# Sliding-window attention with sink tokens into a maxout FFN on one core: more zero products at the start, one cast on ScalarE, and a new order of the first five chunks

## The chip, the cores and the metric

The kernel runs on one core of a Trainium2 chip. The metric is the device time of one execution in microseconds. Before the change three runs took 179.35, 179.66 and 179.69 us, a median of 179.66. Five engines work side by side, each through its own list of instructions in order, and wait for one another by semaphores: PE (TensorE, matrix products; its weight loads are the row PEld), DVE (VectorE), ACT (ScalarE), POOL (GpSimd) and SP (SyncE, which here only issues DMAs).

## The reference

Attention over 4 batches, 8 heads, 768 positions and a head dimension of 64: a query sees the 128 positions up to its own, and the first 4 positions (the sinks). The result, 3072 tokens by 512, goes through an FFN whose hidden layer is the maximum of three products.

```python
scores = scale * np.matmul(q, k.transpose(0, 1, 3, 2))
is_sink = pos[None, :] < int(n_sink)                  # n_sink = 4
rel = pos[:, None] - pos[None, :]
in_window = (rel >= 0) & (rel < int(window))          # window = 128
scores = np.where(is_sink | in_window, scores, -1000000000.0)
a = softmax(scores)
x = np.matmul(a, v)                                   # tokens x 512, heads side by side
h = np.maximum(np.maximum(x @ w1, x @ w2), x @ w3)    # 512 -> 768
out = h @ w_out                                       # 768 -> 512
```

Inputs and output are float32 in device memory; the kernel computes in bf16 with float32 sums.

## The kernel before, in words

**Chunks.** The work is cut into 12 chunks of 256 positions of one batch (3 chunks a batch), each with all 8 heads, taken as 4 pairs of heads. For a chunk the kernel does the following.

- `load` (line 76) brings q, k and v as float32, 512 KB each, by SP's DMA queue. `part` and `parts` cut a load into halves of the heads (head pairs 0 and 1, and 2 and 3). A `gate` is a small POOL write into the target (a memset, or a copy from a weight tile) for which the DMA must wait; so POOL's place in its order decides when the load may be issued. The raw tiles have two buffers a kind.
- `cast_qk` (95) casts one half of q or k to bf16 on the engine that it is given, `cast_v` (104) a quarter of v.
- `turn` (109) and `turn2` (129) transpose one half of q or k on PE, four products with the identity, and copy the result from PSUM to qT or kT on the engine given. From chunk 4 on `turn_dma` (150) does it by DMA.
- `premask` (251) puts an additive mask into the score banks by two products with the identity ahead of the scores; `score` (259) computes the transposed scores of a pair; `expo` (282) takes the exponential on ACT, in two halves; `mask` (289) multiplies by 0 and 1 on DVE where no premask was put. `sink_k`, `sink_score`, `sink_v` (224, 294, 310) treat the four sink positions for chunks 1 and 2 of a batch.
- `av_open` and `av` (324, 338) multiply with v and a column of ones; DVE takes the reciprocal of the sums and scales (355, 358). `xpose` (362) transposes the result for the FFN.
- `ffn_h(ci, fp, wi)` (381) is one group of 8 products: chunk ci, columns 256 fp to 256 fp + 255 of hidden layer matrix wi. For wi = 0 the result is copied to h_sb (397), for 1 and 2 DVE takes the maximum (401). `ffn_y` (407) is the output product, six products of 512 columns, and a copy; `store` writes out.

**The weights** are cast on the way by POOL's own DMA queue, in nine parts of 256 columns (`load_w`, 234) and the output matrix in two (`load_wo`, 242).

**PSUM.** There are 8 banks, handed out first in, first out in the order of the program text (`bank` and `give`, 57 and 63). So the order of the text also decides whose release a bank's next user waits for.

**The order** of the first three chunks and a part of chunks 3 and 4 is written out by hand (454 to 660), call by call; each call adds to the lists of its engines. The chunks behind follow a loop (661). The text's order counts on each engine separately: two calls that share no engine and no bank can change places without a difference.

**Zeros.** `warm(n)` (172) has PE multiply n times a tile of zeros, 512 columns each, into a bank that nobody reads. The kernel does five such products at the start, and four more behind the first turn and premask.

Of the kernel before, what the change touches and what calls it, by code (L numbers as in the profile page):

```python
# [16 lines left out]
def kernel(  # L17
# [13 lines left out]
    nc = tc.nc  # L31
# [17 lines left out]
    with tc.manual_schedule():  # L49
# [13 lines left out]
        def give(*banks):  # L63
            for x in banks:
                free.append(home.pop(id(x))[1])
# [10 lines left out]
        def load(ci, what="kqv", gate=None, part=None, parts=1):  # L76
            if ci >= NCH:
                return
            b, c = divmod(ci, CPB)
            t0 = c * 256  # L80
            for w in what:
                src = {"k": k, "q": q, "v": v}[w]
                if (ci, w) not in raws:
                    raws[ci, w] = raw.tile([128, H, 2, D], F32, tag=w + "_raw", name=w + "_raw")
                dst = raws[ci, w]
                if gate is not None:
                    gate(dst[0:1, 0, 0, 0:1])
                n = H // parts
                for g in range(parts) if part is None else (part,):
                    nc.sync.dma_start(  # L90
                        out=dst[:, n * g:n * g + n],
                        in_=src[b, n * g:n * g + n, t0:t0 + 256]
                            .rearrange("h (p i) d -> p h (i d)", i=2))

        def cast_qk(ci, w, g, eng):

            if (ci, w) not in bfs:
                bfs[ci, w] = raw.tile([128, NP, 2, 2, D], BF16, tag=w + "_bf", name=w + "_bf")
            x, y = bfs[ci, w], raws[ci, w]
            f = eng.copy if eng is nc.scalar else eng.tensor_copy  # L100
            f(x[:, 2 * g:2 * g + 2].rearrange("q p i a d -> q p a i d"),  # L101
              y[:, 4 * g:4 * g + 4].rearrange("q (p a) i d -> q p a i d", a=2))
# [6 lines left out]
        def turn(ci, w, g, eng=None):  # L109

            pt = bank([128, 4, 128], BF16, "pt")
            x = bfs[ci, w]
            for i in range(4):
                y = x[:, 2 * g + i // 2, i % 2]
                nc.tensor.transpose(pt[:, i], y.rearrange("s a d -> s (a d)"), ident)  # L115
            eng = eng or (nc.scalar if w == "q" else nc.vector)
            f = eng.copy if eng is nc.scalar else eng.tensor_copy
            if w == "q":
                f(
                    qT[ci % RING][:, 2 * g:2 * g + 2].rearrange("q p i n r -> q (p i) (n r)"), pt)  # L120
            else:
                f(
                    kT[ci % RING][:, :, 2 * g:2 * g + 2].rearrange("q n p i r -> q n (p i) r"),
                    pt.rearrange("q x (n r) -> q n x r", r=64))
            give(pt)
# [46 lines left out]
        def warm(n):  # L172

            if n:
                pw = bank([128, 512], F32, "warm")
                for _ in range(n):
                    nc.tensor.matmul(pw, lhsT=wz[:, 0:128], rhs=wz, start=True, stop=True)  # L177
                give(pw)
# [103 lines left out]
        def expo(ci, p):  # L282
            lo = 0 if ci % CPB else 1
            e, st = es[ci, p]
            for a in range(2):
                nc.scalar.activation(e[:, a, lo:], st[a][:, lo:], AF.Exp, scale=scale)  # L286
                give(st[a])
# [164 lines left out]


        load(0, 'q', part=1, parts=2)
        warm(5)
        load(0, 'k')
        load(0, 'q', part=0, parts=2)
        load(0, 'v', part=0, parts=2, gate=pool_gate)
        load(0, 'v', part=1, parts=2)
        masks()  # L460
        sink_init()
        factors(msk, addm)
        cast_qk(0, 'q', 1, nc.scalar)
        turn(0, 'q', 1, nc.scalar)
        premask(0, (2,))
        warm(4)
        cast_qk(0, 'k', 1, nc.vector)
        cast_qk(0, 'k', 0, nc.gpsimd)
        cast_qk(0, 'q', 0, nc.gpsimd)
        turn(0, 'k', 1, nc.vector)  # L470
        load(1, 'k')
        premask(0, (3,))
        turn(0, 'k', 0, nc.scalar)
        score(0, (2,))
        score(0, (3,))
        turn(0, 'q', 0, nc.vector)
# [8 lines left out]
        load(1, 'v')  # L485
        score(0, (0,))
        expo(0, 3)
        premask(0, (1,))
        score(0, (1,))
        expo(0, 0)  # L490
        cast_qk(1, 'k', 0, nc.gpsimd)
        load_w(0, 256, 512)
        expo(0, 1)
        av_open(0)
        av(0, 2)
        av(0, 3)
# [3 lines left out]
        cast_qk(1, 'q', 0, nc.gpsimd)  # L500
        cast_qk(1, 'q', 1, nc.scalar)
        turn(1, 'k', 1, nc.scalar)
        av(0, 1)
        premask(1, (0,))
        premask(1, (1,))
        turn2(1, 'q', 0, nc.vector)
        turn(1, 'q', 1, nc.scalar)
        sink_k(0)
        cast_v(1, 0, 0, nc.vector)
        cast_v(1, 1, 0, nc.vector)  # L510
        load_w(0, 0, 256)
        load_w(1, 512, 768)
        score(1, (0,))
        score(1, (1,))
        expo(1, 0)
        expo(1, 1)
        xpose(0, 0, nc.vector)
        xpose(0, 1, nc.vector)
        cast_v(1, 1, 1, nc.gpsimd)
        load_w(1, 256, 512)  # L520
        cast_v(1, 0, 1, nc.gpsimd)
        load_w(1, 0, 256)
        sink_v(0)
        sink_score(1)
        score(1, (3,))
        load(2, 'k', part=0, parts=2, gate=after(0, 300))
        load(2, 'k', part=1, parts=2)
        ffn_h(0, 2, 0, 1, nc.vector)
        expo(1, 3)
        score(1, (2,))  # L530
        expo(1, 2)
        load(2, 'q', part=1, parts=2)
        load(2, 'q', part=0, parts=2, gate=pool_gate)
        load_w(2, 0, 256)
        load_w(2, 256, 512)
        load_w(2, 512, 768)
        mask(1, 3)
        ffn_h(0, 1, 0)
        mask(1, 2)
        av_open(1)  # L540
        cast_qk(2, 'k', 1, nc.gpsimd)
        av(1, 0)
        av(1, 1)
        ffn_h(0, 0, 0)
        load(2, 'v', gate=after(0, 300))
        av(1, 3)
        av(1, 2)
        ffn_h(0, 2, 1)
        ffn_h(0, 1, 1)
        xpose(1, 0, nc.vector)  # L550
        xpose(1, 1, nc.scalar)
        ffn_h(0, 0, 1)
        ffn_h(1, 2, 0)
        cast_qk(2, 'k', 0, nc.scalar)
        ffn_h(1, 1, 0)
        ffn_h(1, 0, 0)
        load_wo()
        load(3, 'q', gate=after(2, 300))
        load(3, 'k')
        factors(msk0, addm0)  # L560
        turn(2, 'k', 0, nc.vector)
        ffn_h(1, 1, 1)
        turn(2, 'k', 1, nc.scalar)
        cast_v(2, 1, 0, nc.gpsimd)
        cast_qk(2, 'q', 1, nc.scalar)
        ffn_h(1, 0, 1)
        cast_qk(2, 'q', 0, nc.vector)
        ffn_h(1, 2, 1)
        turn(2, 'q', 1, nc.scalar)
# [3 lines left out]
        score(2, (0,))  # L573
        expo(2, 0)
        score(2, (3,))
        mask(2, 0)
        score(2, (1,))
        sink_score(2)
        ffn_h(0, 1, 2)
        cast_v(2, 1, 1, nc.gpsimd)  # L580
        load(3, 'v', gate=after(1))
        cast_v(2, 0, 0, nc.gpsimd)
        cast_v(2, 0, 1, nc.gpsimd)
        expo(2, 3)
        expo(2, 1)
        ffn_h(1, 0, 2)
        ffn_h(0, 2, 2)
        ffn_h(1, 2, 2)
        score(2, (2,))
        load(4, 'q', gate=after(0, 300))  # L590
        cast_qk(3, 'q', 0, nc.gpsimd)
        mask(2, 1)
        av_open(2)
        expo(2, 2)
        ffn_y(0, 0)
        load(4, 'k', gate=after(0))
        load(4, 'v')
        cast_qk(3, 'k', 0, nc.gpsimd)
        cast_qk(3, 'k', 1, nc.scalar)
        mask(2, 3)  # L600
        mask(2, 2)
        cast_qk(3, 'q', 1, nc.vector)
        av(2, 0)
        ffn_y(0, 1)
        turn(3, 'q', 0, nc.scalar)
        av(2, 2)
        load(5, 'q')
        av(2, 3)
        turn(3, 'q', 1, nc.scalar)
        load(5, 'k', gate=after(0, 300))  # L610
        av(2, 1)
        ffn_y(1, 0)
        turn(3, 'k', 1, nc.scalar)
# [2 lines left out]
        xpose(2, 1, nc.vector)  # L616
        ffn_y(1, 1)
        cast_qk(4, 'q', 1, nc.vector)
        cast_v(3, 1, 1, nc.gpsimd)
        cast_v(3, 0, 0, nc.gpsimd)  # L620
        cast_v(3, 0, 1, nc.gpsimd)
        score(3, (1,))
        cast_qk(4, 'q', 0, nc.vector)
        expo(3, 1)
        score(3, (0,))
        cast_qk(4, 'k', 1, nc.gpsimd)
        mask(3, 1)
        cast_v(4, 1, 0, nc.gpsimd)
        ffn_h(2, 0, 0)
        cast_qk(4, 'k', 0, nc.vector)  # L630
        score(3, (3,))
        cast_v(3, 1, 0, nc.vector)
        turn_dma(4, 'k')
        turn_dma(4, 'q')
        store(0)
        store(1)
        score(3, (2,))
        expo(3, 0)
        expo(3, 3)
        ffn_h(2, 0, 2)  # L640
        mask(3, 0)
        mask(3, 3)
# [4 lines left out]
        mask(3, 2)  # L647
        av(3, 0)
        av(3, 1)
        ffn_h(2, 2, 0)  # L650
        load(5, 'v', gate=pool_gate)
        ffn_h(2, 1, 1)
        av(3, 3)
        ffn_h(2, 2, 1)
        av(3, 2)
        ffn_h(2, 2, 2)
        cast_v(4, 0, 0, nc.gpsimd)
        cast_v(4, 0, 1, nc.gpsimd)
        cast_v(4, 1, 1, nc.gpsimd)
        ffn_h(2, 1, 2)  # L660
        for i in range(3, NCH):
            n, m = i + 1, i - 1
# [153 lines left out]
```

## Time and profile before

| what | us |
|---|---|
| median of three runs | 179.66 (179.35 to 179.69) |
| the profiled execution | 178.26 |
| its span, first to last instruction | 176.5 |
| PE busy | 168.6 (96%) |
| DVE, ACT, POOL busy | 120.5, 86.4, 66.2 |
| HBM read and written | 25.17 MB and 6.29 MB |

The span is shorter than the execution by what lies ahead of the first and behind the last instruction. Busy times of one engine are those of its work, not of its waits; PE's products overlap, and their ends are modelled. A row of the timeline has the start and the length in us, the engine, the line of the code, the operation with the tile written and the tiles read, the shape, and how many instructions in a row it stands for; in brackets comes the time that the engine was idle before it, and what ended that. The row of a DMA issue is the issuing; a row of the DMA view adds the time from the issue to the landing.

### The profile page before, as it was taken

To read this page: it belongs to the slowest core of one execution; us is meant where nothing else is said; L and a number is where in the kernel's file an instruction comes from. 1 tells how busy PE (TensorE), PEld (TensorE's weight loads), DVE (VectorE), ACT (ScalarE), POOL (GpSimd) and SP (SyncE) were. 2 spreads that over 40 slices of the span, in tenths; PEclk is the share of its full clock that TensorE was granted. 3 is DMA by queue.
4 is the path that set the end of the run, shared out by engine and by line. 5 is a ranking of instruction groups with operands and counts; after the bars stand their busy time and mean duration, and the time that the engine had idled before them with its cause. 6 is when DMAs were issued, how large, how long until landed. Compare 5 with 4: busy or idle time off the path is not lost.

```text
span 176.5 us, 4618 instructions
## 1 busy us (share of the span) xinstructions
PE 168.6 (96%) x1855; PEld 126.5 (72%) x1867; DVE 120.5 (68%) x263; ACT 86.4 (49%) x173; POOL 66.2 (38%) x127
## 2 busy tenths in 40 slices
PE   5978999999999999999999999999999999999992
PEld 1546789867686687597696696796795795796871
DVE  3178764796697895775775874875785775976361
ACT  4197726766953914914724814814616616420210
POOL 7589407455293584074172145244253000000000
PEclk9999999999999999999999999999999999999998
DMA  5999999999999999997998999999999215203203
GB/s 156 297 281 198 204 214 234 217 299 287 290 188 301 304 205 198 262 236 202 258 198 219 251 182 248 260 159 243 276 163 245 32 28 156 119 4 59 119 2 119
DMA packets 70693, 34.90 MB, mean 198 GB/s; under 512 B 26640, under 2 KB 69136, under 8 KB 70672
## 3 DMA queue, kind: packets, MB, share of 16 engines
q1 hardware_dynamic: 64976, 31.33, 79.4%
q0 software_dynamic: 5552, 3.15, 12.6%
q8 instruction: 14, 0.23, 0.6%
q10 hardware_dynamic: 144, 0.13, 0.2%
q14 instruction: 7, 0.06, 0.1%
HBM read 25.17 MB, written 6.29 MB: 178 GB/s over the span
## 4 chain that ended last, share of the span: by engine, by line
PE 85%; DVE 8%; ACT 2%; issue 2%; DMA 2%
PE h_ps L390 49%; PE y_ps L411 17%; PE o L350 6%; PE st L274 6%; DVE h_sb L401 2%; PE pt L115 2%; DVE x_sb L358 2%; DMA q_raw<-in_q_dram 2%; ACT e_sb L286 1%; DVE vb L105 1%; PE o L332 1%; PE warm L177 1%; DVE e_sb L292 1%; PE xt L371 1%; PE y_ps L421 1%
## 5 line engine op out<-in xcount | busy, mean ns | idle before, releaser
L390 PE MATMUL h_ps<-xT,w 128*128 128x256 bf16 x864 | 101.7, 273 | 0.1
L390 PEld LDWEIGHTS <-w 128*128 128x128 bf16 x864 | 81.8, 98 | 10.7 <-issue 0.8
L401 DVE TENSOR_TENSOR h_sb<-h_sb,h_ps 128x512 bf16<-128x512 bf16 (+1 forms) x74 | 49.2, 670 | 17.8 <-PE h_ps L390 16.0
L286 ACT ACTIVATE e_sb<-st 128x512 bf16<-128x512 f32 (+1 forms) x96 | 46.4, 583 | 6.7 <-PE st L274 6.7
L397 ACT CAST h_sb<-h_ps 128x512 bf16<-128x512 f32 x35 | 20.6, 588 | 47.2 <-PE h_ps L390 47.0
L105 POOL CAST vb<-v_raw 64x512 bf16<-64x512 f32 x42 | 27.2, 647 | 19.3 <-DMA v_raw<-in_v_dram 17.9
L411 PE MATMUL y_ps<-wo,h_sb 128*128 128x512 bf16 x126 | 31.9, 380 | 0.6
L292 DVE TENSOR_TENSOR e_sb<-e_sb,msk 128x1024 bf16<-128x1024 bf16 (+1 forms) x42 | 27.0, 679 | 2.8 <-ACT e_sb L286 2.6
L101 POOL CAST k_bf<-k_raw 128x512 bf16<-128x512 f32 x19 | 11.8, 637 | 41.1 <-DMA k_raw<-in_k_dram 32.3
L411 PEld LDWEIGHTS <-h_sb 128*128 128x128 bf16 x138 | 12.4, 98 | 14.4 <-issue 1.6
L358 DVE TENSOR_TENSOR x_sb<-o,rc 128x256 bf16<-128x256 f32 x48 | 20.4, 424 | 1.7
L413 DVE COPY y_sb<-y_ps 128x512 f32<-128x512 f32 x13 | 9.0, 691 | 14.2 <-PE y_ps L411 14.1
L350 PE MATMUL o<-vb,e_sb 128*128 128x65 bf16 x352 | 16.8, 193 | 0.9 <-DVE vb L105 0.9
L350 PEld LDWEIGHTS <-e_sb 128*128 128x128 bf16 x352 | 14.7, 97 | 2.9 <-ACT e_sb L286 1.1
L274 PE MATMUL st<-qT,kT 64*128 64x128 bf16 (+1 forms) x256 | 14.6, 238 | 0.6 <-DVE qT L141 0.4
L274 PEld LDWEIGHTS <-kT 64*128 64x128 bf16 x256 | 8.5, 94 | 7.5 <-issue 5.1
L101 POOL CAST q_bf<-q_raw 128x512 bf16<-128x512 f32 x17 | 10.3, 627 | 5.0 <-DMA q_raw<-in_q_dram 4.9
L355 DVE RECIPROCAL rc<-o 128x4 f32<-128x4 f32 x48 | 8.4, 175 | 4.0 <-PE o L350 3.9
L306 ACT ACTIVATE e_sink<-sk 128x256 bf16<-128x256 f32 x8 | 3.1, 389 | 14.4 <-PE sk L300 14.4
L413 ACT COPY y_sb<-y_ps 128x512 f32<-128x512 f32 x10 | 5.8, 585 | 3.2 <-PE y_ps L411 2.9
L237 POOL DMA_DIRECT2D w<-in_moe_w_dram x9 | 7.0, 786 | 0.0
L177 PE MATMUL warm<-wz 128*128 128x512 bf16 x9 | 4.2, 631 | 1.2 <-DVE wz L166 1.2
(67 smaller groups left out, 71.5 us busy)
## 6 DMA issues: line engine op xcount, KB each, us to landing
k_raw<-in_k_dram SPq DMA_DIRECT2D x11, 512.0 KB, 4.9
v_raw<-in_v_dram SPq DMA_DIRECT2D x11, 512.0 KB, 7.1
out_dram<-y_sb SPq DMA_DIRECT2D x11, 512.0 KB, 3.2
q_raw<-in_q_dram SPq DMA_DIRECT2D x10, 512.0 KB, 6.4
w<-in_moe_w_dram POOLq DMA_DIRECT2D x9, 256.0 KB, 6.4
q_raw<-in_q_dram SPq DMA_DIRECT2D x4, 256.0 KB, 7.4
wo<-in_moe_w_out_dram POOLq DMA_DIRECT2D x2, 384.0 KB, 7.9
v_raw<-in_v_dram SPq DMA_DIRECT2D x2, 256.0 KB, 5.1
```

The lines of the kernel that those rows point to most:

```text
L101: f(x[:, 2 * g:2 * g + 2].rearrange("q p i a d -> q p a i d"), y[:, 4 * g:4 * g + 4].rearrange("q (p a) i d -> q p a i d", a=2))
L105: eng.tensor_copy(vb[ci % RING][64 * i:64 * i + 64, n, :, 0:D], raws[ci, "v"][64 * n:64 * n + 64, :, i])
L274: nc.tensor.matmul(st[a][:, s:s + q1 - q0].rearrange("q n (i r) -> q n i r", i=2), lhsT=x[hp, n, p].rearrange("q i r -> q (i r)"), rhs=qc[ ...
L286: nc.scalar.activation(e[:, a, lo:], st[a][:, lo:], AF.Exp, scale=scale)
L292: (eng or nc.vector).tensor_mul(e[:, :, lo:], e[:, :, lo:], msk0 if lo else msk)
L350: nc.tensor.matmul(o[:, t, a], lhsT=e[:, a, s], rhs=vb[cv % RING][:, n, 2 * p + a], start=first, stop=True, skip_group_check=True)
L358: nc.vector.tensor_mul(xs[ci][:, :, p], o[:, :, :, 0:D], rc.unsqueeze(3).to_broadcast([128, 2, 2, D]))
L390: nc.tensor.matmul(hp[:, f].rearrange("q (i t r) -> q i t r", i=2, t=2), lhsT=w_sb[wi][:, ds, c0:c0 + 128], rhs=xTs[ci][:, :, ds].rearrang ...
L397: (nc.scalar.copy if eng is nc.scalar else eng.tensor_copy)(dst, hp)
L401: nc.vector.tensor_max(dst[:, x], dst[:, x], hp[:, x])
L411: nc.tensor.matmul(yp, lhsT=hs[ci][:, fb, t * 128:(t + 1) * 128], rhs=wo[:, fb], start=(fb == 0), stop=(fb == FB - 1))
L413: (nc.scalar.copy if eng is None else eng.tensor_copy)(ys[ci][:, t], yp)
```

## The change

It makes the first group of zeros eight products instead of five, and puts the second group ahead of the mask products of pair 2 instead of behind them. The first half of chunk 0's k is cast on ScalarE instead of GpSimd, and turned ahead of the mask products of pair 3. The rest are changes of place: casts, turns, sink steps, weight loads, exponentials, AV products, groups of h and y of chunks 0 to 4. Everything else, the loop behind included, is the same. On PE the three zeros are the only instructions more; SP's list is the same.

```diff
         load(0, 'q', part=1, parts=2)
-        warm(5)
+        warm(8)
...
         load(0, 'v', part=0, parts=2, gate=pool_gate)
+        cast_qk(0, 'q', 1, nc.scalar)
         load(0, 'v', part=1, parts=2)
...
-        cast_qk(0, 'q', 1, nc.scalar)
         turn(0, 'q', 1, nc.scalar)
+        warm(4)
         premask(0, (2,))
-        warm(4)
+        cast_qk(0, 'k', 0, nc.scalar)
         cast_qk(0, 'k', 1, nc.vector)
-        cast_qk(0, 'k', 0, nc.gpsimd)
-        cast_qk(0, 'q', 0, nc.gpsimd)
         turn(0, 'k', 1, nc.vector)
         load(1, 'k')
+        turn(0, 'k', 0, nc.scalar)
+        cast_qk(0, 'q', 0, nc.gpsimd)
         premask(0, (3,))
-        turn(0, 'k', 0, nc.scalar)
...
+        load_w(0, 0, 256)
         av(0, 1)
         premask(1, (0,))
+        turn2(1, 'q', 0, nc.vector)
+        sink_k(0)
         premask(1, (1,))
-        turn2(1, 'q', 0, nc.vector)
         turn(1, 'q', 1, nc.scalar)
-        sink_k(0)
         cast_v(1, 0, 0, nc.vector)
         cast_v(1, 1, 0, nc.vector)
-        load_w(0, 0, 256)
         load_w(1, 512, 768)
+        xpose(0, 0, nc.vector)
         score(1, (0,))
         score(1, (1,))
         expo(1, 0)
         expo(1, 1)
-        xpose(0, 0, nc.vector)
+        load_w(1, 256, 512)
+        cast_v(1, 1, 1, nc.gpsimd)
         xpose(0, 1, nc.vector)
-        cast_v(1, 1, 1, nc.gpsimd)
-        load_w(1, 256, 512)
         cast_v(1, 0, 1, nc.gpsimd)
         load_w(1, 0, 256)
-        sink_v(0)
+        score(1, (3,))
         sink_score(1)
-        score(1, (3,))
         load(2, 'k', part=0, parts=2, gate=after(0, 300))
         load(2, 'k', part=1, parts=2)
+        sink_v(0)
+        expo(1, 3)
         ffn_h(0, 2, 0, 1, nc.vector)
-        expo(1, 3)
...
         av_open(1)
-        cast_qk(2, 'k', 1, nc.gpsimd)
+        ffn_h(0, 0, 0)
         av(1, 0)
-        av(1, 1)
-        ffn_h(0, 0, 0)
         load(2, 'v', gate=after(0, 300))
         av(1, 3)
+        av(1, 1)
         av(1, 2)
...
         ffn_h(0, 0, 1)
+        cast_qk(2, 'k', 1, nc.gpsimd)
         ffn_h(1, 2, 0)
         cast_qk(2, 'k', 0, nc.scalar)
+        ffn_h(1, 0, 0)
         ffn_h(1, 1, 0)
-        ffn_h(1, 0, 0)
...
         turn(2, 'k', 0, nc.vector)
+        ffn_h(1, 0, 1)
+        cast_v(2, 1, 0, nc.gpsimd)
+        turn(2, 'k', 1, nc.scalar)
         ffn_h(1, 1, 1)
-        turn(2, 'k', 1, nc.scalar)
-        cast_v(2, 1, 0, nc.gpsimd)
         cast_qk(2, 'q', 1, nc.scalar)
-        ffn_h(1, 0, 1)
...
+        ffn_y(0, 0)
+        ffn_y(0, 1)
         av(2, 0)
-        ffn_y(0, 1)
         turn(3, 'q', 0, nc.scalar)
+        cast_qk(3, 'k', 1, nc.scalar)
...
         score(3, (0,))
+        cast_qk(4, 'k', 0, nc.vector)
         cast_qk(4, 'k', 1, nc.gpsimd)
         mask(3, 1)
+        ffn_h(2, 0, 0)
         cast_v(4, 1, 0, nc.gpsimd)
-        ffn_h(2, 0, 0)
-        cast_qk(4, 'k', 0, nc.vector)
```

More of the change, by code (lines that the diff above doesn't have):

```diff
@@ L487 @@
         expo(0, 3)
+        cast_qk(1, 'k', 0, nc.gpsimd)
         premask(0, (1,))
@@ L490 @@
         expo(0, 0)
-        cast_qk(1, 'k', 0, nc.gpsimd)
+        expo(0, 1)
         load_w(0, 256, 512)
-        expo(0, 1)
         av_open(0)
@@ L534 @@
         load_w(2, 0, 256)
+        expo(1, 2)
         load_w(2, 256, 512)
@@ L575 @@
         score(2, (3,))
-        mask(2, 0)
         score(2, (1,))
+        cast_v(2, 1, 1, nc.gpsimd)
         sink_score(2)
         ffn_h(0, 1, 2)
-        cast_v(2, 1, 1, nc.gpsimd)
+        expo(2, 1)
+        mask(2, 0)
         load(3, 'v', gate=after(1))
         cast_v(2, 0, 0, nc.gpsimd)
+        expo(2, 3)
+        ffn_h(1, 0, 2)
         cast_v(2, 0, 1, nc.gpsimd)
-        expo(2, 3)
-        expo(2, 1)
-        ffn_h(1, 0, 2)
         ffn_h(0, 2, 2)
@@ L591 @@
         cast_qk(3, 'q', 0, nc.gpsimd)
+        av_open(2)
+        load(4, 'k', gate=after(0))
         mask(2, 1)
-        av_open(2)
         expo(2, 2)
-        ffn_y(0, 0)
-        load(4, 'k', gate=after(0))
+        cast_qk(3, 'k', 0, nc.gpsimd)
         load(4, 'v')
-        cast_qk(3, 'k', 0, nc.gpsimd)
-        cast_qk(3, 'k', 1, nc.scalar)
         mask(2, 3)
@@ L602 @@
         cast_qk(3, 'q', 1, nc.vector)
+        ffn_y(0, 0)
+        ffn_y(0, 1)
         av(2, 0)
-        ffn_y(0, 1)
         turn(3, 'q', 0, nc.scalar)
+        cast_qk(3, 'k', 1, nc.scalar)
+        load(5, 'q')
         av(2, 2)
-        load(5, 'q')
+        load(5, 'k', gate=after(0, 300))
         av(2, 3)
         turn(3, 'q', 1, nc.scalar)
-        load(5, 'k', gate=after(0, 300))
         av(2, 1)
@@ L618 @@
         cast_qk(4, 'q', 1, nc.vector)
-        cast_v(3, 1, 1, nc.gpsimd)
         cast_v(3, 0, 0, nc.gpsimd)
@@ L622 @@
         score(3, (1,))
+        cast_v(3, 1, 1, nc.gpsimd)
         cast_qk(4, 'q', 0, nc.vector)
@@ L625 @@
         score(3, (0,))
+        cast_qk(4, 'k', 0, nc.vector)
         cast_qk(4, 'k', 1, nc.gpsimd)
         mask(3, 1)
+        ffn_h(2, 0, 0)
         cast_v(4, 1, 0, nc.gpsimd)
-        ffn_h(2, 0, 0)
-        cast_qk(4, 'k', 0, nc.vector)
+        cast_v(3, 1, 0, nc.vector)
         score(3, (3,))
-        cast_v(3, 1, 0, nc.vector)
         turn_dma(4, 'k')
@@ L636 @@
         store(1)
-        score(3, (2,))
         expo(3, 0)
         expo(3, 3)
+        score(3, (2,))
         ffn_h(2, 0, 2)
@@ L649 @@
         av(3, 1)
-        ffn_h(2, 2, 0)
         load(5, 'v', gate=pool_gate)
         ffn_h(2, 1, 1)
+        ffn_h(2, 2, 0)
         av(3, 3)
@@ L656 @@
         ffn_h(2, 2, 2)
-        cast_v(4, 0, 0, nc.gpsimd)
         cast_v(4, 0, 1, nc.gpsimd)
         cast_v(4, 1, 1, nc.gpsimd)
+        cast_v(4, 0, 0, nc.gpsimd)
         ffn_h(2, 1, 2)
```

1 line of the change is left out of this document (removed).

## The prediction

> **What bounds the kernel now.** I read the windows first, then the timeline of the first 32 us, then the chain of waits. The windows (busy time by engine, then granted clock, DMA share, GB/s):
>
> ```profile
> 5.00:13.00 8.00, 6.82 (x66) 3.74 (x65) 3.82 (x10) 4.95 (x12) 5.51 (x11) 1.00 1.22 289
> 13.00:20.00 7.00, 6.49 (x99) 4.46 (x97) 5.31 (x15) 5.84 (x13) 6.50 (x11) 1.00 1.44 193
> 18.50:57.00 38.50, 38.32 (x458) 30.01 (x458) 28.97 (x63) 23.39 (x48) 18.27 (x34) 1.00 1.19 249
> 57.00:172.00 115.00, 114.53 (x1250) 87.52 (x1258) 81.13 (x167) 51.28 (x103) 33.15 (x56) 1.00 0.83 179
> ```
>
> From 18.5 us on PE idles for 0.2 us of 38.5, and after that for 0.5 of 115: time can be won or lost only ahead of 18.5, or by a new stall behind it. The DMA share is over 1 through the first 57 us, so the loads flow without a break there, and a load lands when all that was queued ahead of it is through. PE and the loads are two limits close together. Now the start, by the timeline (start, length, engine, line, what; in brackets the idle time before and its releaser):
>
> ```profile
> 1.20 2.32 PE L177 MATMUL warm<-wz 128*128 128x512 bf16 x5 [1.20 <-DVE wz L166]
> ...
> 3.78 0.62 ACT L101 CAST q_bf<-q_raw 128x512 bf16<-128x512 f32 x1 [1.54 <-DMA q_raw<-in_q_dram]
> ...
> 4.45 0.61 PE L115 MATMUL pt<-ident,q_bf 128*128 128x128 bf16 x4 [0.94 <-ACT q_bf L101]
> ...
> 5.10 0.58 ACT L119 COPY qT<-pt 128x512 bf16<-128x512 bf16 x1 [0.70 <-PE pt L115]
> ...
> 5.50 1.91 PE L177 MATMUL warm<-wz 128*128 128x512 bf16 x4
> ...
> 5.54 0.43 DVE L101 CAST k_bf<-k_raw 128x512 bf16<-128x512 f32 x1 [1.73 <-DMA k_raw<-in_k_dram]
> ...
> 5.57 0.86 POOL L101 CAST k_bf<-k_raw 128x512 bf16<-128x512 f32 x1 [0.37 <-DMA k_raw<-in_k_dram]
> ...
> 6.49 0.61 POOL L101 CAST q_bf<-q_raw 128x512 bf16<-128x512 f32 x1
> ...
> 7.20 0.63 PE L115 MATMUL pt<-ident,k_bf 128*128 128x128 bf16 x4
> ...
> 8.22 0.39 PE L115 MATMUL pt<-ident,k_bf 128*128 128x128 bf16 x4
> ...
> 8.40 0.61 POOL L105 CAST vb<-v_raw 64x512 bf16<-64x512 f32 x1 [1.30 <-DMA v_raw<-in_v_dram]
> ...
> 9.41 0.42 DVE L119 COPY qT<-pt 128x512 bf16<-128x512 bf16 x1 [1.11 <-PE pt L115]
> ...
> 9.75 1.93 DVE L105 CAST vb<-v_raw 64x512 bf16<-64x512 f32 x3
> ...
> 11.82 0.53 PE L350 MATMUL o<-vb,e_sb 128*128 128x65 bf16 x12 [0.90 <-DVE vb L105]
> ...
> 11.91 0.61 POOL L101 CAST q_bf<-q_raw 128x512 bf16<-128x512 f32 x1 [0.46 <-DMA q_raw<-in_q_dram]
> ...
> 13.27 1.03 PE L256 MATMUL st<-addm,ident 128*128 128x512 bf16 x4
> ...
> 14.74 0.41 DVE L141 COPY qT<-pt 128x512 bf16<-128x512 bf16 x1
> ...
> 15.07 0.94 DVE L105 CAST vb<-v_raw 64x512 bf16<-64x512 f32 x2
> ...
> 16.19 0.76 DVE L372 COPY xT<-xt 128x512 bf16<-128x512 bf16 x2 [0.18 <-PE xt L371]
> ...
> 17.25 1.03 PE L390 MATMUL h_ps<-xT,w 128*128 128x256 bf16 x8
> ```
>
> Four products of 512 columns take 1.91 us at 5.50 and 1.03 us at 13.27, so PE begins at half pace, though the clock column reads 1.00. The two k turns (7.20 and 8.22, 0.63 against 0.39) put the change of pace near 8.15, 3.7 us after PE's gap before 4.45. That gap is the one the change fills.
>
> The Trainium skill, "TensorE: Matmul & The Clock Gate", Part 1, says that PE's clock opens after a busy window of about 3.4 us, that the windows run free, and that the moment so varies from run to run. The 3.7 us fit it; one trace can't show the variation.
>
> **The start, worked out.** Eight products at (5.50 to 7.20)/4 = 0.427 us reach from 1.20 to 4.6: q's first turn comes 0.15 later than at 4.45, and the gap is gone. By the same 3.7 us, full pace comes at 4.9. Then turn 0.25 and four zeros 0.9 to about 5.8, the two mask products 0.32 to 6.1, k's second half (cast by 5.97) turned by 6.3. K's first half goes to ScalarE, behind the qT copy, which moves with q's turn from 5.10 to some 5.2 and ends near 5.8; at 0.62 (ScalarE's q row) it is ready at 6.4, as on POOL (5.57 + 0.86), and its turn is done by 6.7, against 8.6. POOL's q cast waits for its load and stays at 6.49 to 7.10. The scores of pairs 2 and 3 follow at 7.1, q's turn at 7.5, its copy on DVE at 7.9 to 8.3, against 9.41 to 9.83. The three v casts then start at once, since v has landed by 8.4 (POOL's row), and end at 10.3 instead of 11.68: the first AV product moves from 11.82 to 10.4, **1.4 us earlier**.
>
> Chunk 1's q lands just ahead of 11.91, whatever PE does. Its cast ends at 12.52; its turn, now ahead of half of the mask products, follows at 12.6, its copy at about 13.0 to 13.5 against 14.74. Then come two v casts (0.94) and two xT copies (0.76), to some 15.3. The first h group, moved behind a bank that the first pair's exponentials free, starts near 15.6 instead of 17.25: **1.6 us ahead**.
>
> **What gives it back.** The loads that PE meets next, by the timeline,
>
> ```profile
> 16.42 0.74 POOL L237 DMA_DIRECT2D w<-in_moe_w_dram  x1
> ...
> 19.01 1.62 SPq L90 DMA_DIRECT2D q_raw<-in_q_dram  x2
> ...
> 23.79 1.40 PE L390 MATMUL h_ps<-xT,w 128*128 128x256 bf16 x11
> ...
> 27.68 0.37 SPq L90 DMA_DIRECT2D v_raw<-in_v_dram  x1
> ...
> 29.32 0.62 ACT L101 CAST q_bf<-q_raw 128x512 bf16<-128x512 f32 x1
> ...
> 30.39 0.39 PE L115 MATMUL pt<-ident,q_bf 128*128 128x128 bf16 x4
> ...
> 30.82 0.43 DVE L101 CAST q_bf<-q_raw 128x512 bf16<-128x512 f32 x1 [0.35 <-DMA q_raw<-in_q_dram]
> ...
> 31.48 0.39 PE L115 MATMUL pt<-ident,q_bf 128*128 128x128 bf16 x4
> ...
> 37.82 1.47 PE L411 MATMUL y_ps<-wo,h_sb 128*128 128x512 bf16 x5
> ```
>
> and of the DMA view the one issue between 16.3 and 16.9, with its KB and us to landing:
>
> ```profile
> w<-in_moe_w_dram POOLq DMA_DIRECT2D x1, 256.0 KB, 6.5
> ```
>
> The last third of the second weight matrix (columns 0 to 255) is issued at 16.42 and lands 6.5 later, at 22.9; PE uses it at 23.79, so 0.85 is left of the lead. Chunk 2's q halves are cast at 29.32 to 29.94 and 30.82 to 31.25, their turns run at 30.39 and 31.48: 0.4, then 0.2 us of slack. The second cast waited for its load, and nothing in the change brings that load forward: POOL issues the weights back to back between 11.9 and 17.2 (busy 6.50 of 7 us), and in the new order it has the same casts, copies and issues to do there, so chunk 2's loads are released at the same time. The turn at 31.48 can come at 31.3 at best: **of 1.6 us, 0.2 stays** of this execution. The span would be 176.3, the time 178.06 against 178.26.
>
> **The other edits**, at nothing each. K and q casts and turns of chunks 1 to 4 and y of chunk 0 change places inside a stretch in which PE idles 0.2 us of 38.5; PE's sum of products doesn't change but for the three zeros, which lie in the gap. The cover: two y groups now stand together ahead of the AV products, from 37.8; both read the h that the first reads at 37.82 already, and the second's bank is freed by a maximum that ended at 38.07, 1.0 us before its place. If such a cover were gone, one DVE maximum (0.69) would show on PE. The cast of k(4) goes ahead of a mask multiplication that waits for an exponential anyway; 0 to 0.1 is won. I take 0 of 0 to -0.1, and up to +0.7 as the other end.
>
> ```profile
> 37.38 0.69 DVE L401 TENSOR_TENSOR h_sb<-h_sb,h_ps 128x512 bf16<-128x512 bf16 x1 [0.19 <-PE h_ps L390]
> ...
> 46.91 0.56 DVE L292 TENSOR_TENSOR e_sb<-e_sb,msk 128x768 bf16<-128x768 bf16 x1 [1.60 <-ACT e_sb L286]
> ```
>
> **From this execution to the median.** The profiled execution took 178.26 (span 176.5 and 1.76 around it), the three runs 179.35 to 179.69. I carry a surplus of 1.40 over, but not all of it: if PE's full pace comes later in those runs, PE is later there while the loads aren't, and the new order removes that lateness, as it holds PE at the loads' limit. What lateness can cost is seen in the chain of waits, behind the change of pace and ahead of the point where DVE's v casts take over:
>
> ```profile
> 8.38 0.22 PE pt L115 x4
> 8.60 0.44 PE st L274 x8
> 9.04 0.34 PE pt L115 x4
> ```
>
> These 1.0 us would take up to twice as long: 0 to 1.0 us. No row says where between; I take the middle, 0.5. **The sum: 179.66 - 0.2 - 0.5 = 179.0 us.**
>
> By the skill's rule the pace changes 3.4 to 6.8 us after the last gap: at 7.9 to 11.3 before (the profiled 8.15 is early), at 4.6 to 8.0 after. That rule would make the 0.5 likely, and a lucky phase in the new kernel worth nothing more.
>
> **Rivals.**
> 1. The lead is kept: were the loads not the limit (chunk 2's q landing over 1.3 us earlier), the 1.6 us would stay, 178.0. The DMA share of 1.2 to 1.4 up to 31 us speaks against it.
> 2. No change: the surplus of the runs has nothing to do with pace, or full pace comes late in the new kernel too (at 8.0, the zeros, masks and turns at half pace end at 8.2 as now). Then 0 to 0.2 stays: 179.5.
> 3. Slower: chunk 2's v load is released on POOL ahead of k's second cast, and so issued near 20.7 instead of 27.68, right behind q (19.01 to 20.63), while POOL's third matrix is in flight. If its 512 KB are served among q's packets and not behind them, they cost at 289 GB/s up to 1.8 us; past 0.2 us of delay, PE stalls at 31.48. The whole of it: the cast at 30.8 + 1.8, its 0.43 and the turn at 33.05, a loss of 1.6, 181.2; half of it, 180.4. Against it: four loads of one queue are expected to land in the order of issue.
> 4. The change doesn't do what it says: PE's pace doesn't follow the gap. Half pace to 8.15 gives rival 2's time.
>
> **How the numbers follow.** Forecast 0.40, rival 1 0.13, rivals 2 and 4 together 0.24, rival 3 (or a stall of 0.7 from the moved edits, 180.2) 0.23. The range 178.0 to 180.4 reaches from rival 1 to half of rival 3 and leaves out about 0.15 on the two sides. A measurement of this kernel tells some 0.2% (0.36 us) from no change. Faster: forecast and rival 1, 0.53; same: 0.24; slower: 0.23.
>
> **What would show it.** Right: no gap of PE ahead of q's first turn, the second group of four zeros in about 1.0 us instead of 1.91, the first AV product near 10.4, the first h group near 15.6, then waits on PE for w at 22.9 and for q at 29.9 and 31.3, and the same order of work behind. Wrong: zeros still at 1.9 us (rival 4), the q turns clearly ahead of 31.2 (rival 1), DVE's q cast behind 31.0 (rival 3), or idle time of PE over 0.3 us behind 32.

## The result, and the profile after

The changed kernel takes 178.31 us, the kernel before 179.68 (179.33 to 180.13), both medians of six runs. One of the six of the changed kernel took 958.66 us, which the ratio leaves out; the other five took 177.9 to 178.5, with a median of 178.23. The ratio is 0.9932, with a 95% interval of 0.9904 to 0.9961: faster by 1.2 us, 0.7 to 1.7. The profiled execution took 178.00, with a span of 176.2; the profiled execution of before took 178.26, which is less than any of the six runs beside it, and than any of the 116 that the experiments add (178.40 at the least). So between the two profiles the difference is only 0.26 us, and most of the gain of the runs can't be read from this pair. That is what the experiments are for.

The windows of the changed kernel (busy time by engine, granted clock, DMA share, GB/s), the same four stretches as before:

```profile
5.00:13.00 8.00, 6.50 (x79) 3.60 (x77) 4.92 (x14) 6.24 (x14) 4.77 (x8) 1.00 1.22 289
13.00:20.00 7.00, 6.76 (x107) 5.00 (x108) 5.14 (x11) 6.07 (x13) 6.86 (x14) 1.00 1.45 197
18.50:57.00 38.50, 37.97 (x447) 29.29 (x446) 27.54 (x62) 22.99 (x47) 18.68 (x34) 1.00 1.18 252
57.00:172.00 115.00, 114.29 (x1251) 87.43 (x1258) 81.47 (x167) 50.76 (x102) 33.26 (x56) 1.00 0.84 178
```

PE now idles for 0.5 us of the 38.5 where it had idled for 0.2, and for 0.7 of the last 115 where it had been 0.5. It arrives earlier and waits more. The DMA share is as it was (1.22, 1.45, 1.18), so nothing here says that the loads have become quicker. The timeline of the changed kernel (start, length, engine, line, what, idle time before and its releaser) shows where:

```profile
1.20 3.59 PE L177 MATMUL warm<-wz 128*128 128x512 bf16 x8 [1.20 <-DVE wz L166]
...
4.59 0.63 PE L115 MATMUL pt<-ident,q_bf 128*128 128x128 bf16 x4
...
5.02 1.19 PE L177 MATMUL warm<-wz 128*128 128x512 bf16 x4
...
8.15 0.42 DVE L119 COPY qT<-pt 128x512 bf16<-128x512 bf16 x1 [0.93 <-PE pt L115]
...
8.68 1.62 DVE L105 CAST vb<-v_raw 64x512 bf16<-64x512 f32 x3
...
10.44 0.53 PE L350 MATMUL o<-vb,e_sb 128*128 128x65 bf16 x12 [0.77 <-ACT e_sb L286]
...
15.99 1.03 PE L390 MATMUL h_ps<-xT,w 128*128 128x256 bf16 x8
...
23.69 2.52 PEld L390 LDWEIGHTS <-w 128*128 128x128 bf16 x24 [0.38 <-DVE xT L372]
...
27.18 0.61 POOL L101 CAST k_bf<-k_raw 128x512 bf16<-128x512 f32 x1 [7.12 <-DMA k_raw<-in_k_dram]
...
27.85 0.40 PE L115 MATMUL pt<-ident,k_bf 128*128 128x128 bf16 x4 [0.26 <-POOL k_bf L101]
...
29.83 0.39 PE L115 MATMUL pt<-ident,q_bf 128*128 128x128 bf16 x4
...
30.61 0.43 DVE L101 CAST q_bf<-q_raw 128x512 bf16<-128x512 f32 x1 [0.70 <-POOL msk L210]
...
31.10 0.40 PE L115 MATMUL pt<-ident,q_bf 128*128 128x128 bf16 x4
...
45.75 0.43 DVE L101 CAST k_bf<-k_raw 128x512 bf16<-128x512 f32 x1 [0.81 <-DMA k_raw<-in_k_dram]
...
46.53 0.56 DVE L292 TENSOR_TENSOR e_sb<-e_sb,msk 128x768 bf16<-128x768 bf16 x1 [0.36 <-ACT e_sb L286]
...
46.68 3.46 SPq L159 DMA_TRANSPOSE kT<-k_bf  x2
...
68.83 0.29 PE L300 MATMUL sk<-qT,ks 128*32 128x256 bf16 x4 [0.24 <-DMA qT<-q_bf]
```

Two rows of the kernel before that the prediction didn't show belong beside these:

```profile
28.42 0.39 PE L115 MATMUL pt<-ident,k_bf 128*128 128x128 bf16 x4
...
69.07 0.29 PE L300 MATMUL sk<-qT,ks 128*32 128x256 bf16 x4
```

Read downwards against the rows of before. The eight zeros run without a gap into q's first turn; the second four zeros take 1.19 us instead of 1.91, so the pace doubles inside the first of them, near 5.3; the first AV product is 1.38 us ahead (10.44 against 11.82) and the first h group 1.26 (15.99 against 17.25). Then the lead shrinks at each load: k's second half has a lead of 0.57 at its turn (27.85 against 28.42), q's last turn 0.38 (31.10 against 31.48), chunk 5's sink scores 0.24 (68.83 against 69.07, the row that the experiments come back to). The chain of waits of the changed kernel names the first of these loads:

```profile
18.13 8.90 DMA k_raw<-in_k_dram
...
27.18 0.62 POOL k_bf L101
...
27.85 0.40 PE pt L115 x4
```

In the chain of the whole span PE had 85% before and has 72% now, and DMA has 15%: the chain now runs through a load where it had run through PE.

### The profile page after: what moved, and what is told of

Read it like the earlier page. It is cut to its first block, busy times and chain, and to the rows that moved or that the text cites. A ratio compares the mean times of both kernels' runs of the same rounds, so it can differ in the third digit from the quotient of the medians.

```text
span 176.2 us, 4621 instructions
## 1 busy us (share of the span) xinstructions
PE 168.6 (96%) x1858; PEld 125.9 (71%) x1870; DVE 120.3 (68%) x263; ACT 87.3 (50%) x174; POOL 65.9 (37%) x126
## 4 chain that ended last, share of the span: by engine, by line
PE 72%; DMA 15%; POOL 8%; issue 2%; SPq 1%; ACT 0%; DVE 0%; POOLq 0%
PE h_ps L390 43%; PE y_ps L411 16%; DMA k_raw<-in_k_dram 9%; PE st L274 5%; PE o L350 5%; DMA v_raw<-in_v_dram 3%; DMA qT<-q_bf 3%; POOL vb L105 2%; POOL w L237 2%; POOL k_bf L101 1%; PE pt L115 1%; PE o L332 1%; PE y_ps L421 1%; SPq L90 1%; PE sk L300 1%
## 5 line engine op out<-in xcount | busy, mean ns | idle before, releaser
L101 POOL CAST q_bf<-q_raw 128x512 bf16<-128x512 f32 x17 | 10.3, 626 | 6.5 <-DMA q_raw<-in_q_dram 6.5
L177 PE MATMUL warm<-wz 128*128 128x512 bf16 x12 | 4.8, 559 | 1.2 <-DVE wz L166 1.2
```

## The experiments

My theory after the result was that of the prediction: the zeros start full pace earlier, the loads take most of the lead back, and in ordinary runs a later start of the pace before leaves some half a microsecond to win. The rival: the moves behind the start, which I had put at nothing, carry the gain. Each kernel was run 12 times, beside 23 or 35 runs of the kernel before on the same chip (medians 179.44 to 179.72); the row of the change is the result above. Differences are the ratio of each pair times 179.6. That ratio is not the quotient of the two medians, which can lie half a microsecond from it: by the medians the later moves alone are 0.95 us faster, the change without the early v 1.24, the one cast 0.22. Of the thirteen differences, those of the start's order (+0.5), of the one cast (-0.4) and of chunk 2's moves (+0.5) have intervals that clear nothing by less than 0.1, and should be read so. Marks are from one profiled execution of each, in us from the start of the span: when PE's pace doubles, the first AV product, chunk 2's last q turn, chunk 5's sink scores, and the span.

| kernel | us | difference, 95% | pace | AV | q turn | sinks | span |
|---|---|---|---|---|---|---|---|
| before | 179.4 to 179.7 | | 8.15 | 11.82 | 31.48 | 69.07 | 176.49 |
| after | 178.31 | -1.2 (-1.7 to -0.7) | 5.3 | 10.44 | 31.10 | 68.83 | 176.23 |
| zeros alone | 179.14 | -0.4 (-0.8 to 0.0) | 4.3 | 10.63 | 32.84 | 70.56 | 177.97 |
| after, five zeros | 178.78 | -0.5 (-1.0 to 0.0) | 8.9 | 12.15 | 32.07 | 69.46 | 176.88 |
| start's order alone | 179.98 | +0.5 (0.1 to 0.9) | 8.15 | 11.40 | 32.39 | 70.70 | 178.11 |
| later moves alone | 178.75 | -0.7 (-1.1 to -0.4) | 9.8 | 12.37 | 32.24 | 70.00 | 177.41 |
| v of chunk 2 early alone | 179.62 | +0.2 (-0.1 to 0.5) | 8.2 | 11.70 | 32.12 | 70.36 | 177.75 |
| after, v not early | 178.36 | -0.7 (-1.2 to -0.2) | by 4.7 | 10.41 | 31.59 | 69.00 | 176.40 |
| after, a weight load behind k | 178.60 | -0.8 (-1.2 to -0.4) | 4.5 | 10.50 | 30.60 | 69.12 | 176.55 |
| zeros and v early | 178.96 | -0.7 (-1.2 to -0.2) | 5.0 | 10.44 | 31.84 | 69.44 | 176.84 |
| later moves, first part | 179.26 | -0.3 (-0.7 to 0.2) | 9.5 | 12.47 | 32.50 | 70.26 | 177.68 |
| later moves, second part | 178.81 | -0.7 (-1.1 to -0.2) | 7.3 | 11.35 | 31.94 | 69.35 | 176.75 |
| one cast of chunk 4 alone | 179.22 | -0.4 (-0.8 to -0.1) | 9.3 | 12.32 | 32.30 | 70.48 | 177.90 |
| chunk 2's moves alone | 180.15 | +0.5 (0.1 to 1.0) | 9.1 | 12.29 | 32.71 | 71.07 | 178.47 |

Two things stand in the columns before any single run is discussed. The span less the sinks' mark is 107.39 to 107.43 in all fourteen rows: what lies behind chunk 5's sink scores is a constant, and every difference between these profiles is made ahead of 71.1 us. And the sinks' mark follows the q turn's by 37.4 to 38.5, whatever the pace column says: a kernel with an early pace and a late q turn (zeros alone) has a long span.

**Zeros alone, and the change without the added zeros.** The first is the kernel before with one number changed, the second the changed kernel with that number put back.

```diff
-        warm(5)
+        warm(8)
```

> The kernel before with three more zero products and nothing else. Pace theory (the gap ahead of q's first turn delays PE's full pace, by an amount that varies from run to run; the loads of chunk 2 set the floor): full pace near 5, the start ahead, nearly the whole gain: 178.3 to 178.7 us, a span of 176.2 to 176.7. Order theory (the moved calls make the gain, the zeros only fill idle time): 179.4 to 179.8, no different from before.

> The changed kernel with five zeros at the start again. Pace theory: PE has its gap of about 1 us back, full pace comes between 7.9 and 11.3, and the time goes back by half or more: 178.8 to 179.5. Order theory: 178.2 to 178.5 as with eight.

Measured: 179.14 us and 178.78 us, differences of -0.4 and -0.5, both with intervals that just reach nothing. The first lies in neither theory's range; the second lies at the lower end of the pace theory's. The timeline of the kernel with the zeros alone:

```profile
1.20 3.43 PE L177 MATMUL warm<-wz 128*128 128x512 bf16 x8 [1.20 <-DVE wz L166]
4.47 0.39 PE L115 MATMUL pt<-ident,q_bf 128*128 128x128 bf16 x4
...
5.02 1.03 PE L177 MATMUL warm<-wz 128*128 128x512 bf16 x4
6.55 0.40 PE L115 MATMUL pt<-ident,k_bf 128*128 128x128 bf16 x4 [0.51 <-DVE k_bf L101]
...
10.63 0.53 PE L350 MATMUL o<-vb,e_sb 128*128 128x65 bf16 x12 [0.77 <-DVE vb L105]
...
28.91 0.40 PE L115 MATMUL pt<-ident,k_bf 128*128 128x128 bf16 x4 [0.51 <-POOL k_bf L101]
...
32.84 0.40 PE L115 MATMUL pt<-ident,q_bf 128*128 128x128 bf16 x4 [0.55 <-DVE q_bf L101]
```

And of the changed kernel with five zeros:

```profile
1.20 2.31 PE L177 MATMUL warm<-wz 128*128 128x512 bf16 x5 [1.20 <-DVE wz L166]
4.49 0.61 PE L115 MATMUL pt<-ident,q_bf 128*128 128x128 bf16 x4 [0.98 <-ACT q_bf L101]
4.89 1.91 PE L177 MATMUL warm<-wz 128*128 128x512 bf16 x4
...
7.24 1.06 PE L115 MATMUL pt<-ident,k_bf 128*128 128x128 bf16 x8
...
12.15 0.53 PE L350 MATMUL o<-vb,e_sb 128*128 128x65 bf16 x12 [0.87 <-ACT e_sb L286]
```

The three zeros by themselves do what was claimed for the pace: with them the first turn is at full pace already (0.39) and the first AV product 1.2 us ahead; without them the gap of 0.98 is back, the four zeros take 1.91 and AV comes at 12.15, 1.7 us behind the changed kernel's. But in the run with the zeros alone chunk 2's second q half landed at 32.26 instead of the 30.73 of the profile of before, PE stands at 28.91 and 32.84, and the span is 1.5 us longer than that of the profiled before. The lead of 1.2 us at AV was worth nothing in that execution, since the load came later.

**The start's order alone, and the later moves alone.** The first is the kernel before, five zeros kept, with the order of the first casts, turns and masks of the changed kernel; the second is the complement, the changed kernel with the start of before.

```diff
+        cast_qk(0, 'q', 1, nc.scalar)
         load(0, 'v', part=1, parts=2)
...
+        warm(4)
         premask(0, (2,))
-        warm(4)
+        cast_qk(0, 'k', 0, nc.scalar)
         cast_qk(0, 'k', 1, nc.vector)
-        cast_qk(0, 'k', 0, nc.gpsimd)
```

> The kernel before with the changed order up to the turn of k's first half (second zeros ahead of the masks, k's first half cast on ScalarE), five zeros as before. Pace theory: the gap stays, so 179.2 to 179.8. Order theory: this is where the path of the start lies, so 178.5 to 179.0.

> The start of the kernel before (five zeros, k cast on GpSimd) and all later moved calls. Pace theory: the gap stays, 179.2 to 179.8. Order theory, if the later moves carry it: 178.3 to 179.0.

Measured: 179.98 us, slower by 0.5 and outside both ranges, and 178.75, faster by 0.7, as the order theory had it. This is the finding of the study: the part that I had put at nothing brings, with a start no different from before and a pace that came late (9.8), about half of the gain or more. The parts don't add up to the whole: zeros -0.4, start's order +0.5 and later moves -0.7 make -0.6 where the change has -1.2, but each of the four is known to some 0.4 or 0.5 us, and the difference lies within that. The timeline of the kernel with the start's order alone shows two waits further on:

```profile
32.39 0.40 PE L115 MATMUL pt<-ident,q_bf 128*128 128x128 bf16 x4 [0.51 <-DVE q_bf L101]
...
70.70 0.29 PE L300 MATMUL sk<-qT,ks 128*32 128x256 bf16 x4 [0.65 <-DMA qT<-q_bf]
```

and that of the kernel with the later moves alone has neither, though its q load (30.73) and its start are no better than those of the profile of before:

```profile
32.24 0.39 PE L115 MATMUL pt<-ident,q_bf 128*128 128x128 bf16 x4
...
70.00 0.29 PE L300 MATMUL sk<-qT,ks 128*32 128x256 bf16 x4
```

The second wait is for the transposed q of chunk 5, which comes by DMA from SP's queue. I hadn't looked so far along.

**Chunk 2's v load.** The change releases it on POOL at 20.66 instead of 27.68, by moving k's second cast behind the release (my third rival). Three kernels: before with that exchange, after without it, and before with it and the eight zeros.

```diff
         av_open(1)
-        cast_qk(2, 'k', 1, nc.gpsimd)
         av(1, 0)
...
         ffn_h(0, 0, 1)
+        cast_qk(2, 'k', 1, nc.gpsimd)
         ffn_h(1, 2, 0)
```

> The kernel before with one exchange on POOL: the release of chunk 2's v load ahead of the cast of chunk 2's k, as in the changed kernel; nothing else differs on any engine. Load theory (what the later moves bring is this: v is queued some 7 us sooner, the DMA engines stay full around 28 to 32 us, and the loads that PE meets there and behind come earlier): 0.5 to 1.0 us less than before, 178.7 to 179.2. Rival (the gain of the later moves lies in chunks 0 and 1, on PE, DVE and ACT): no different, 179.5 to 179.9.

> The changed kernel with that one exchange undone: k's cast ahead of the release of chunk 2's v load. Load theory: 0.4 to 1.0 us more than the changed kernel, 178.7 to 179.3. Rival: as the changed kernel, 178.2 to 178.5.

> The kernel before with eight zeros and the one exchange on POOL, none of the other moves. If the two together are the change: 178.2 to 178.6, as the changed kernel. If the other moves carry a part: 178.7 to 179.2.

Measured: 179.62 us (+0.2), 178.36 (-0.7 against before) and 178.96 (-0.7). The early release alone changes nothing that can be told; undone in the changed kernel, the gain stays, with an interval that overlaps the full change's; with the zeros, the pair stands at -0.7 where the zeros alone have -0.4, well within the intervals. No gain or loss that can be told comes from it. Issued at 20.86 in the first of the three, v landed at 33.46, behind q's second half at 31.55. Over all the profiles q's second half landed between 29.30 and 32.14 in the eight kernels with the early v, and between 30.73 and 32.26 in the six with the late one, so nothing shows that v pushes it back.

**A weight load moved behind the k cast.** If the loads ahead of 31 us take the lead back, a third of the last hidden matrix issued later should bring them forward. The changed kernel with

```diff
-        load_w(2, 512, 768)
         mask(1, 3)
...
         cast_qk(2, 'k', 1, nc.gpsimd)
+        load_w(2, 512, 768)
         ffn_h(1, 2, 0)
```

> The changed kernel with the last third of the third weight matrix issued behind the cast of chunk 2's k instead of ahead of the release of v, so that it no longer shares the DMA engines with chunk 2's k and q. If those loads are the floor that takes back PE's lead (waits at 27.8 and 31.1 us), k and q land about 1 us sooner, the waits shrink and up to 0.8 us of the lead stays: 177.3 to 178.0. If the floor is elsewhere, or comes back at once with w_out and chunk 3's loads: 178.2 to 178.6.

Measured: 178.60 us, no better than the change. The timeline of this kernel:

```profile
27.52 0.40 PE L115 MATMUL pt<-ident,k_bf 128*128 128x128 bf16 x4
...
30.60 0.39 PE L115 MATMUL pt<-ident,q_bf 128*128 128x128 bf16 x4
...
69.12 0.29 PE L300 MATMUL sk<-qT,ks 128*32 128x256 bf16 x4 [0.42 <-DMA qT<-q_bf]
```

The wait at 27.85 is gone, q's second half landed at 29.30, and PE turns it 0.5 us ahead of the changed kernel. At 69.12 it waits for the transposed q of chunk 5 all the same. In this execution there are two gates in a row, and the lead that passed the first was gone at the second.

**The later moves in two parts.** All of the later moves up to the AV products of chunk 1, and all behind.

```diff
+        load_w(0, 0, 256)
         av(0, 1)
         premask(1, (0,))
+        turn2(1, 'q', 0, nc.vector)
...
+        expo(1, 3)
         ffn_h(0, 2, 0, 1, nc.vector)
```

> The kernel before with the later moves up to the AV products of chunk 1 only (weights issued ahead of sink_k and of the v cast on POOL, turn, xpose, scores and banks of chunks 0 and 1); start, five zeros and all behind as before. If the gain of the later moves (some 0.85 us of the rest-only kernel) comes from chunks 0 and 1, by weights and loads that land sooner: 178.6 to 179.0. If from behind: 179.4 to 179.8.

> The kernel before with the later moves from the AV products of chunk 1 on only (order of h groups, release of v, turns of chunk 2, casts and y of chunks 2 to 4; on DVE k of chunk 4 is cast ahead of a mask, so SP's transposes are released sooner). If the gain of the later moves comes from here, by the second place where PE waits for loads (near 70 us, for the transposed q of chunk 5): 178.6 to 179.0. If from chunks 0 and 1: 179.4 to 179.8.

Measured: 179.26 us (-0.3, not told from nothing, and between the two ranges) and 178.81 (-0.7, as much as all the later moves bring). So the gain sits in the main behind 20 us, in the moves of chunks 2 to 4; the two intervals overlap, and a share of the first part isn't excluded.

**One cast of chunk 4, and chunk 2's moves.** In the kernel before DVE casts the first half of chunk 4's k behind a mask multiplication that waits for an exponential; SP's DMA transposes wait for that cast, and chunk 5's loads and transposes stand behind them on SP's queue. Over the profiles, those transposes start 1.9 to 2.3 us behind the landing of chunk 4's k in the seven kernels with the old place, and 1.0 us behind it in six of the seven with the new one (1.7 in the other). So the cast was tried alone, and beside it the moves of the second part up to chunk 2's last turn. (Chunk 4's k landed at 45.79 in the profile of before and at 45.66 in that of the change; the transposes of the change stand above, at 46.68.)

```diff
+        cast_qk(4, 'k', 0, nc.vector)
         cast_qk(4, 'k', 1, nc.gpsimd)
         mask(3, 1)
         cast_v(4, 1, 0, nc.gpsimd)
         ffn_h(2, 0, 0)
-        cast_qk(4, 'k', 0, nc.vector)
```

> The kernel before, with one call moved: DVE casts the first half of chunk 4's k ahead of the mask multiplication of chunk 3's second pair instead of behind it. On every other engine the list stays as it is. Theory A (the cast is what the moves behind the second chunk's AV bring): SP's DMA transposes of chunk 4 and all that stands behind them on SP's queue start 1.2 us earlier (46.7 instead of 47.9 in the profile), the transposed q of chunk 5 lands clearly ahead of PE's wait near 69 to 70.5 us in every execution, and the stall of 0.7 to 0.8 us that the runs with only the new start and with the early v showed there goes: 178.9 to 179.2 us beside 179.6 to 179.7 of the kernel before. Theory B (the gain is in chunk 2's places, ahead of 32 us): the transposes start earlier just the same, but PE reaches chunk 5's sink scores no earlier: 179.5 to 179.8 us.

> The kernel before, with the moves from chunk 1's AV bank to chunk 2's last turn alone: the casts, turns and v load of chunk 2, and the h groups and AV products between them; what lies behind (chunk 2's scores onwards) as before. Theory A (the cast of chunk 4's k brings the gain): no difference, 179.5 to 179.8 us. Theory B (chunk 2's places bring it): 178.8 to 179.2 us, with the last turn of chunk 2's q on PE no later than 32.0 us in the profile. If neither this kernel nor the one with the cast alone is faster, what remains are the moves of chunks 2 and 3 between them, and the two would read 179.5 to 179.8 both.

Measured: 179.22 us for the cast, faster by 0.4 (0.1 to 0.8; 0.22 by the medians), and 180.15 for chunk 2's moves, slower by 0.5 and outside both ranges. Theory B falls: chunk 2's places don't bring the gain. Theory A has its direction, barely clear of nothing; its reason isn't borne out by the profiles, as shown below. The timeline of the kernel with the cast alone:

```profile
47.64 0.43 DVE L101 CAST k_bf<-k_raw 128x512 bf16<-128x512 f32 x1 [1.02 <-DMA k_raw<-in_k_dram]
47.98 0.96 DVE L292 TENSOR_TENSOR e_sb<-e_sb,msk 128x768 bf16<-128x768 bf16 x1
...
48.57 3.50 SPq L159 DMA_TRANSPOSE kT<-k_bf  x2
...
61.59 4.16 SPq L159 DMA_TRANSPOSE kT<-k_bf  x2
...
70.48 0.29 PE L300 MATMUL sk<-qT,ks 128*32 128x256 bf16 x4 [0.54 <-DMA qT<-q_bf]
```

In this execution the k load itself landed at 47.55, 1.8 us later than in the profile of before, so the early cast waited for it, the transposes started at 48.57, and the stall at 70.48 was there. The place of the cast takes 1.1 us out of the chain behind the load; it can't bring the load.

How far does that 1.1 us reach? The rows of the kernel before, with the last line of the view of SP's transposes of q up to 72 us (the second of three is chunk 5's):

```profile
47.88 2.59 SPq L159 DMA_TRANSPOSE kT<-k_bf  x2
...
64.22 1.26 SPq L154 DMA_TRANSPOSE qT<-q_bf  x1
...
DMA to landing us min/median/max: 3.2/3.2/3.4
```

and those of the change:

```profile
63.81 1.26 SPq L154 DMA_TRANSPOSE qT<-q_bf  x1
...
DMA to landing us min/median/max: 3.2/3.3/5.0
```

Chunk 4's transposes start 1.2 us earlier, chunk 5's q is issued only 0.4 earlier, and it lands 1.4 later, at 68.78 instead of 67.38, since this one transpose took 5.0 us instead of 3.2. So before the change q was there 1.7 us ahead of PE, which came at 69.07; after it PE waits. Over the fourteen profiles the wait at the sinks stands in six (the change, the start's order, v early alone, the weight load behind k, the cast alone, chunk 2's moves), and there chunk 5's q took 4.5 to 5.0 us; in the other eight it took 3.1 to 3.2 and was there 1.7 to 2.9 us ahead of PE. The wait is in three of the seven kernels with the old place of the cast and in three of the seven with the new. What goes with it is the next transpose on SP's queue, that of x (line 377): it was issued 1.98 to 2.42 us behind q's in the six, 2.55 to 3.76 in the eight. Whether the one makes the other, no run here shows.

The time from PE's last turn of chunk 2's q to the sinks, without the wait, was 37.64 us in the kernel with the cast alone, and 37.59 to 37.76 in the seven with the old place. So if the cast's 0.4 us is real, the wait must be rarer or shorter with it, and one profile of each kernel can't show that.

What stays open is by which road the later moves gain. The cast has -0.4, chunk 2's moves have +0.5, and the second part as a whole -0.7. Unless the parts act on one another, the moves between (chunk 2's masks, exponentials and AV, and the releases of the loads of chunks 4 and 5) bring the rest, near 0.8, with an uncertainty about as large. They weren't tried by themselves.

## Why the prediction came out as it did

The predicted 179.0 us stands 0.7 above the result, which lies inside the range, near its lower end; faster was the likelier side. That it lies inside is in part luck: about half of the gain comes from edits that the sum had at nothing.

**The bound** was right: PE and the loads, close together. The changed kernel's chain goes through DMA for 15% of the span.

**The pace** was right. Full pace was put at 4.9 and came near 5.3; it follows the gap, which settles rival 4. Over the fourteen profiles the five kernels with eight zeros have it at 4.3 to 5.3, the nine with five zeros at 7.3 to 9.8. A spread of 2.5 us fits a window of some 3.4 us that runs free, as the Trainium skill states it ("TensorE: Matmul & The Clock Gate", Part 1). The working of the prediction by that rule, 3.4 us behind the gap at the earliest, doesn't hold: in the kernel with the second part of the later moves the gap ended at 4.59 and the pace changed at 7.3, 2.7 us behind it.

**The start, worked out**, was right up to the first AV product: q's copy at 8.15 (7.9 forecast), v casts done at 10.30 (10.3), the product at 10.44 (10.4), though by its row the exponentials were the last to release it, not the v casts. The first h group came at 15.99 instead of 15.6, a lead of 1.26 for 1.6.

**What gives it back** was right in size, with one gate more than named. The last third of the second weight matrix landed at 22.50 (22.9 forecast) and PE didn't wait for it; k's second half, which I hadn't named, did hold PE at 27.85; q's turns came at 29.83 and 31.10 (29.9 and 31.3). Of the profiled execution 0.26 us was won; 0.2 was forecast.

**The surplus of the median** was too small, and its reason doesn't fit. The runs lay 1.42 us above the profiled execution before and lie 0.31 above it after, so 1.1 us of surplus went where the sum took 0.5. I took it for lateness of PE that the loads don't share, and zeros alone are worth 0.4, with an interval down to nothing. But the loads vary too: the profile of before has the earliest first k load of all fourteen (5.51; the others 5.62 to 6.22), and chunk 2's last q half landed from 29.30 to 32.26. The step "PE is later there while the loads aren't" meets its counterexample in the profile of the zeros alone, in which PE was early and the loads late. How much of the surplus is the loads', one profile of the kernel before can't show.

**The other edits, at nothing**, is the step that was wrong. They bring 0.7 us (0.4 to 1.1), where the prediction allowed them a tenth at most and put the far end of their range at a loss of 0.7. I costed them on PE, in a stretch in which PE idled 0.2 us, and one sentence gave the cast of k(4) "0 to 0.1" because the mask behind it waits anyway. That is true of the mask, but the cast has another consumer, SP, whose transposes went from 47.88 to 46.68. That this is where the 0.4 us of the cast come from is not shown: in the two profiles 0.4 of the 1.2 is left where chunk 5's q is issued, and the wait of 0.24 to 0.69 us at the sinks stands in as many profiles with the new place as with the old. In the profile that I read there was no such wait, and q lay there 1.7 us early. So the runs show which edits gain; how they gain stays open.

**Rival 3** (v's early load delays q) cost nothing that can be told: the load was issued at 20.66 and q's second half landed at 30.52, against 30.73 before. The objection beside it, that loads of one queue land in the order of issue, is what the traces show for these: in all fourteen v landed behind q's second half, by 1.6 us at the least. **Rival 1** (the lead is kept) is out for the start's lead, which shrank to 0.24; the time of 178.3 comes near its 178.0 by another way.

## What to carry to other kernels

Cost a moved instruction at every engine that waits for its result, a DMA queue too, and then follow the lead along that queue: here 1.2 us at its start were 0.4 a few transfers further on, and gone at the landing. If the runs of a kernel lie above its profiled execution, the profile is a lucky one: it can be without a wait that other executions pay, even where it shows 1.7 us to spare, so take a second profile before building on it. A lead that is won ahead of a row of loads is worth what the last of them leaves. And test the edits that a forecast puts at nothing as a group: here they brought half of the gain or more.

## What the runs showed of the hardware

- Loads land at other times in each execution: over the fourteen profiles, each of another kernel, the first k load (512 KB), issued at 1.26 or 1.27 in each, landed between 5.51 and 6.22, and chunk 2's second q half (256 KB), issued between 19.29 and 21.74, between 29.30 and 32.26.
- The granted clock of the profile reads 1.00 while PE runs at half pace: 1.00 in the stretch from 5 to 13 us of the kernel before, in which four products of 512 columns took 1.91 us and, later in the same trace, 1.03.
- With three products of zeros more, 1.3 us of PE, the change of pace came in a narrow place (4.3 to 5.3 in five profiles); with the gap of about 1 us ahead of the first turn it came anywhere from 7.3 to 9.8 (nine).
- The DMA transpose of chunk 5's q took either 3.1 to 3.2 us from issue to landing (eight profiles) or 4.5 to 5.0 (six), with nothing between, and PE waited for it in those six alone.
